# First batch in single query tiles, weight conversion spread from step 0, and the MLP's queue reordered, in a fused top-k attention and MLP kernel

## The chip, the cores and the metric

The kernel runs on one core of one Trainium2 chip. The metric is the device time of one execution in microseconds (us), and the time of the kernel before is the median of three runs. All steps and lines below name the kernel before, where nothing else is said.

## The reference, cut to what matters

```python
# q, k, v: (8 batches, 8 heads, 576 rows, 64)
scores = 0.125 * q @ k.T                      # 576 x 576 per head
kth = 32nd largest of each row
attn = softmax(where(scores >= kth, scores, -1e9))
x = (attn @ v), heads side by side            # (8, 576, 512)
xn = (x - mean) / sqrt(var + 1e-6) * g_ln     # over the 512
out = x + relu(xn @ w_ch1) @ w_ch2            # 512 -> 2048 -> 512
```

The weights arrive as 64-bit floats and are converted to 32 bits inside the kernel. All matrix products are in 32-bit floats; each appears in the trace as two matmul records and two weight loads.

## The kernel before, in words

The attention is cut into 160 **units**. A unit is one batch, one pair of heads and one tile of query rows. The 576 rows of a batch give four full tiles of 128 rows (numbers 0 to 3) and a last one of 64 (number J = 4, the "rest"). A full unit has two score tiles, one for each head; a rest unit packs both heads into one.

The units of one head pair and one set of query tiles form a **job**. The tiles of a job are one **group**: its product with the values (`values`, L487 and L494) is made at once, when the last unit is through. A batch has eight jobs: four head pairs for a first half of its tiles, then four for the second. Batch 0 has tiles 0, 1 and then 2, 3, J; the other batches have 0, 1, J and then 2, 3. So units 0 to 7 are full, and so on.

A loop runs over **steps** n. The instructions are written out by hand in that order, and each engine runs its own in that order (`manual_schedule`). In step n these run:

- TensorE (PE): scores of unit n+1 (L362), transposes of the weights of unit n-2 (L434, L463; L454, L455 for a rest), the values product of a group that ended with unit n-3, the transposes of its result (L526, `place`), and MLP work.
- VectorE (DVE): the 32 largest of unit n in four rounds of `select` (L379 max, L384 match-replace), the turning of heads (L321, `turn_heads`), the reciprocals of the softmax sums (L782).
- GpSimd (POOL): the mask of unit n-1 (L409, L412). While weights are converted, units are **shared** with ScalarE: then tile 0 of the unit gets its mask from two ScalarE activations (L399, L400) and one POOL operation (L407).
- ScalarE (ACT): copies of the scores from PSUM (L345), exponentials of unit n-2 (L419), copies and scalings.
- SyncE (SP): the DMA queue, in order.

**Weight conversion.** The weights are 32 pieces of 128x512: 16 of `w_ch1` (four column blocks `nb` with four pieces each) and then 16 of `w_ch2`. A piece goes through `fetch` (DMA), `split` (three ACT activations L168 to L172 and a POOL clamp L173), `shift` (DVE, L176) and `join` (two POOL operations, L182 and L183). When a column block is whole, `mean_of` (PE, L212) and `centre` (DVE, L223) fold the layer norm's mean and gain into it. `weights(n, phase)` is called at phases 0 to 3 of a step. Four pieces come ahead of the loop, then two with each step, and from step 10 one. `mean_of` is in phase 3, the end of a step, so it stands on PE ahead of the scores of the next step.

**The MLP.** Query tiles whose heads are all done make a **block** (mostly two tiles). `Block.items()` gives its work: `turn_x` (transposes of x, L576, copy L581), 64 `hidden` products (L589, as wide as the block) with an activation (L601) for each four, and 16 `project` products for each tile (L606, 512 wide). A block is handed over (`give`) four steps after its last unit. `give` first runs all that is left of the earlier blocks, then sets a plan: the block's cost is spread over the steps up to the next block. `fill()` has eight places in a step and puts as much of the list there as the plan allows.

Blocks are given at step 11, then 23, 35, 43, 55, 63, 75 and so on. The rests of two batches make a full tile of 128 rows; the rests of batches 0 to 3 make a block of two such tiles, given together with the block of step 75, and those of batches 4 to 7 one with the block of step 155. These two steps so hand over four tiles.

`NV` is the number of buffers of values (`v`, `ends`). `hpool` has 15 buffers of 128x512, for the conversion's temporaries and the activated hidden layer.

Of the kernel before, what the change touches and what calls it, by code (L numbers as in the profile page):

```python
# [20 lines left out]
J = 4  # L21
# [7 lines left out]
def kernel(  # L29
# [50 lines left out]

    NV = 3
    GQ = 2 * P + R
# [17 lines left out]
    xtpool = pool("xt", 1)  # L100
    hpool = pool("h", NF - 1)
    psps = pool("ps", 5, space=PSUM)
# [29 lines left out]
    class Piece:  # L132
# [26 lines left out]
        def split(self):  # L159
            def tmp(name, dt):  # L160
                return hpool.tile([P, DM], dt, tag="h", name=name)

            high = self.raw[:, :, 1].bitcast(FP32)
            self.size = tmp("size", U32)
            self.low = tmp("low", FP32)
            self.sign = tmp("sign", FP32)
            size_f = self.size[:].bitcast(FP32)
            nc.scalar.activation(size_f, high, AF.Abs)  # L168
            nc.scalar.activation(
                self.low[:], self.raw[:, :, 0], AF.Copy, bias=2.0, scale=2.0**-51  # L170
            )
            nc.scalar.activation(self.sign[:], high, AF.Sign)  # L172
            nc.gpsimd.tensor_scalar(size_f, size_f, HIGH_MAX, HIGH_MIN, ALU.min, ALU.max)  # L173
# [6 lines left out]
        def join(self):  # L180
            size = self.size[:]
            nc.gpsimd.tensor_tensor(size, size, self.low[:].bitcast(U32), ALU.add)  # L182
            nc.gpsimd.tensor_tensor(  # L183
                self.dst, size.bitcast(FP32), self.sign[:], ALU.mult
            )
            ready[self.i] = True

    ready = [False] * (2 * NF)
    centred = [False] * (DFF // DM)
    pieces = [Piece(i) for i in range(2 * NF)]  # L190
    gmat = [None]
    means = {}

    def load_gain():
        grow = const([NC, P], "grow")
        nc.scalar.dma_start(grow[:], g_ln.rearrange("(c p) -> c p", p=P))
        ps = turned()
# [22 lines left out]
    def centre(nb):  # L220
        for c in range(NC):
            w = w1[:, c, nb * DM : (nb + 1) * DM]
            nc.vector.scalar_tensor_tensor(  # L223
                out=w, in0=w, scalar=gcol[:, c : c + 1], in1=means[nb][:],
                op0=ALU.mult, op1=ALU.subtract,
            )
        centred[nb] = True

# [3 lines left out]
    for n in range(-1, 2 * NF):  # L232
        size = 4 if n < 0 else 2 if n < 10 else 1
        batches[n], queue = queue[:size], queue[size:]

    def weights(n, phase):

        now, before = batches.get(n, []), batches.get(n - 1, [])
        done = [x.i // NC for x in before if x.i < NF and x.c == NC - 1]
        if phase == 0:  # L240
            for x in batches.get(n + 1, []):
                x.fetch()
            for x in now[0::2]:
                x.split()
        elif phase == 1:
            for x in before:
                x.shift()
            for x in before[0::2]:
                x.join()
        elif phase == 2:  # L250
            for x in now[1::2]:
                x.split()
            for x in before[1::2]:
                x.join()
            for nb in means:
                if not centred[nb]:
                    centre(nb)
        elif phase == 3:
            for nb in done:
                mean_of(nb)  # L260

# [4 lines left out]
    owed = [0.0]  # L266

    def pop():
        cost, run, may = todo.pop(0)
        assert not may or may()  # L270
        owed[0] -= cost
        run()

    def fill():
        owed[0] = min(owed[0] + share[0], 6.0)
        while todo and owed[0] >= todo[0][0] / 2 and (not todo[0][2] or todo[0][2]()):
            pop()
# [9 lines left out]

    def load(job, other):

        job.ins = {}  # L290
        for name, src, queue in (("k", k, nc.sync), ("q", q, other)):
            t = ldpool.tile([P, S], FP32, tag=name + "in", name=name + "in")
# [46 lines left out]
    def scores(u):  # L339

        u.sc = scpool.tile([P, 2, S], FP32, tag="sc", name="sc")
        made = [score_half(u, s) for s in range(2)]
        for s, pss in enumerate(made):
            for t, ps in enumerate(pss):
                nc.scalar.copy(u.sc[:, t, s * HALF : (s + 1) * HALF], ps[:, 0:HALF])  # L345

# [191 lines left out]
    class Block:  # L538
# [25 lines left out]
        def items(self):  # L564
# [6 lines left out]
            def turn_x(i):  # L571
                if i == 0:
                    xT[0] = xtpool.tile([P, NC, 2 * P], FP32, tag="xT", name="xT")
                tp = turned()
# [28 lines left out]
            def project(i, f):  # L603
# [9 lines left out]
                if f == NF - 1:  # L613
# [5 lines left out]

            per_row = 1.75e-3  # L620
            out = [(0.66, lambda i=i: turn_x(i), None) for i in range(n)]
            out += [
                (
                    max(per_row * N, 0.31),
                    lambda f=f, c=c: hidden(f, c),
                    lambda f=f: centred[f * P // DM],
                )
                for f in range(NF)
                for c in range(NC)
            ]  # L630
            out += [
                (
                    per_row * DM,
                    lambda i=i, f=f: project(i, f),
                    lambda f=f: ready[NF + f] and (f < NF - 1 or self.ready),
                )
                for i in range(n)
                for f in range(NF)
            ]
            return out  # L640


# [5 lines left out]
    for b in range(B):  # L648
        lo, hi = list(range(J // 2)), list(range(J // 2, J))
        (lo if b else hi).append(J)  # L650
        for qts in (lo, hi):
            jobs += [Job(b, hp, [qts]) for hp in range(NHP)]
# [31 lines left out]
    for j in jobs:  # L684
        if j.hp == NHP - 1:
            b = j.b
            rest = J in j.groups[0].qts
            step = j.last + 4
            tiles = [(b, qt) for g in j.groups for qt in g.qts if qt < J]
            add_block(step, tiles, [[(out[b, t[1] * P : (t[1] + 1) * P, :], full)] for t in tiles])  # L690
            if b % 4 == 3 and rest:
                rests = [("r", b // 2 - 1), ("r", b // 2)]
                add_block(
                    step,
                    rests,
                    [
                        [
                            (out[2 * r, JP:S, :], slice(0, R)),
                            (out[2 * r + 1, JP:S, :], slice(R, P)),
                        ]  # L700
                        for _, r in rests
                    ],
                )

    SLOTS = 8
# [4 lines left out]
    turns = {}  # L710
    for j in fresh[1:]:
        before = jobs[jobs.index(j) - 1]
        turns[before.first] = j

# [20 lines left out]
    def give(n):  # L735
        while todo:
            pop()
        owed[0] = 0.0
        for blk in gives[n]:
            todo.extend(blk.items())  # L740
        after = [m for m in gives if m > n]
        steps = range(n, min(after) if after else END)
        need = sum(t[0] for t in todo)
        kappa = (need + sum(map(pe_cost, steps))) / sum(map(dve_cost, steps))
# [5 lines left out]

    load(fresh[0], nc.scalar)
    weights(-2, 0)
    turn_heads(fresh[0])
    load(fresh[1], nc.sync)
    scores(units[0])
    load_gain()
    load_values(jobs[0])
    weights(-1, 0)
    weights(-1, 2)
    recips = {}  # L760
    for n in range(END):
        if n in gives:
            give(n)
# [4 lines left out]
        late = late if late and late.rest and late.job.b % 2 else None  # L768
        if u and n == u.job.first and n > 0:
            load_values(u.job)  # L770
        parts = turn(ex) if ex else []
# [3 lines left out]
        if nxt:  # L775
            scores(nxt)
        if g:
            values(g)
        if u:
            select(u, 0)  # L780
        for den in recips.pop(n, []):
            nc.vector.reciprocal(den, den)  # L782
        if mk:
            prepare(mk)
            mask(mk, 0)
        weights(n, 0)
# [10 lines left out]
        if n in turns:  # L797
            turn_heads(turns[n])
            later = fresh.index(turns[n]) + 1
            if later < len(fresh):  # L800
                load(fresh[later], nc.sync)
        for blk in gives.get(n - 1, []):
            blk.std()
        if mk and len(mk.tiles) > 1:
            mask(mk, 1)
        weights(n, 1)
# [9 lines left out]
        if u:  # L816
            select(u, 2)
        for blk in gives.get(n - 1, []):
            blk.inverse()
        if ex and ex.group.last == n - 2:  # L820
            whole = [qt for qt in ex.group.qts if qt < J]
            den = ex.group.den[:, 2 * whole[0] : 2 * whole[-1] + 2]
            nc.gpsimd.tensor_scalar_add(den, den, DEN_EPS)
            recips.setdefault(n + 1, []).append(den)
        last_rest = at(n - 3)
# [7 lines left out]
        if parts:  # L833
            parts[-1]()
        fill()
        if u:
            select(u, 3)
# [5 lines left out]
        if late and late.job.hp == NHP - 1:  # L843
            r = late.job.b // 2
            blk, i = block_of["r", r]
            blk.stats(i, rs[r])
        weights(n, 3)
        fill()
# [33 lines left out]
```

## Time and profile before

| what | value |
|---|---|
| median of three runs | 1771.33 us (1771.23 to 1772.55) |
| profiled execution, device time | 1770.78 us |
| its span | 1768.3 us |
| PE busy | 1635.9 us (93%) |
| VectorE busy | 1521.8 us (86%) |
| GpSimd busy | 1208.3 us (68%) |
| ScalarE busy | 969.3 us (55%) |
| PE busy in the first 242 us | 145.9 us |
| VectorE's last unit ends | 1638.5 us |

The span is the profiler's, and 2.5 us of the execution lie around it. A matmul's end is modelled by the profiler, so that PE's work is best read from the starts of records in the timeline. Where a step begins on VectorE is read from the start of the first max over fresh scores of its unit. Where a block begins on PE is read from the first record of L576.

### The profile page before, as it was taken

What the parts mean: (1) busy time and instruction counts of PE and PEld (TensorE: products, weight loads), DVE (VectorE), ACT (ScalarE), POOL (GpSimd) and SP (SyncE); (2) the same over time, 40 slices, a digit from 0 to 9 for tenths busy, and PEclk for the clock granted to TensorE, in tenths of its full rate; (3) what the DMA queues carried; (4) which work ended last, traced back from release to release, by engine and by line L of the source; (5) the groups of instructions that cost most, each with busy time, mean ns of one, the idle gap of its engine ahead of it and who ended that gap; (6) DMA issues with size and microseconds to landing.
All of it is one profiled execution on the core that took longest, in us unless ns stands there. A gap on an engine that the chain in (4) does not pass through costs nothing.

```text
span 1768.3 us, 23805 instructions
## 1 busy us (share of the span) xinstructions
PE 1635.9 (93%) x7617; PEld 1034.6 (59%) x7617; DVE 1521.8 (86%) x3162; ACT 969.3 (55%) x2563; POOL 1208.3 (68%) x959
## 2 busy tenths in 40 slices
PE   3555999999999999999999999999999999999998
PEld 1223746657574757575756575647575756566765
DVE  7888999999999999996569999999999999996000
ACT  4658876556564646553356565656565646544411
POOL 4869787787777777873467877777778776883300
PEclk9677999999999999999999999999999999999999
DMA  7423112101210012001021012101120021000000
GB/s 173 103 69 97 54 31 51 28 26 28 46 28 20 24 37 54 20 14 38 15 39 28 26 28 53 21 20 27 34 53 21 20 40 34 14 26 14 6 13 12
DMA packets 244485, 65.53 MB, mean 37 GB/s; under 512 B 235653, under 2 KB 235657, under 8 KB 244361
## 3 DMA queue, kind: packets, MB, share of 16 engines
q1 hardware_dynamic: 241984, 63.73, 16.2%
q8 instruction: 60, 0.98, 0.2%
q10 hardware_dynamic: 2376, 0.30, 0.1%
q14 instruction: 65, 0.52, 0.1%
HBM read 54.53 MB, written 9.44 MB: 36 GB/s over the span
## 4 chain that ended last, share of the span: by engine, by line
DVE 41%; PE 35%; POOL 9%; issue 9%; ACT 5%; DMA 1%; POOLq 0%; SPq 0%; DVEq 0%; ACTq 0%
DVE m L379 21%; DVE wk L384 18%; PE hps L589 13%; PE ops L606 11%; PE scps L362 4%; PE av L487 3%; PE tp L434 3%; POOL e L409 2%; POOL w L183 2%; POOL size L182 2%; POOL e L412 2%; ACT sc L345 1%; POOL e L407 1%; PE av L494 1%; POOL size L173 1%
## 5 line engine op out<-in xcount | busy, mean ns | idle before, releaser
L409 POOL TENSOR_SCALAR e<-sc,m 128x576 f32<-128x576 f32 x270 | 598.2, 2215 | 239.4 <-DVE m L379 170.9
L379 DVE MAX8 m<-wk 128x8 f32<-128x576 f32 x864 | 612.6, 746 | 2.1
L589 PE MATMUL hps<-xT,w 128*128 128x256 f32 x2304 | 556.9, 385 | 27.5 <-ACT xT L581 27.5
L606 PE MATMUL ops<-w,h 128*128 128x512 f32 x1152 | 544.0, 596 | 0.0
L589 PEld LDWEIGHTS hps<-xT,w 128*128 128x128 f32 x2304 | 419.5, 192 | 93.8 <-ACT xT L581 31.8
L384 DVE MATCH_REPLACE8 wk<-m,wk 128x576 f32<-128x576 f32 x576 | 423.7, 742 | 0.0
L412 POOL TENSOR_TENSOR e<-e,sc 128x576 f32<-128x576 f32 x270 | 380.3, 1409 | 22.6
L606 PEld LDWEIGHTS ops<-w,h 128*128 128x128 f32 x1152 | 199.3, 191 | 162.5 <-issue 157.4
L419 ACT ACTIVATE e<-e,bias 128x576 f32<-128x576 f32 x288 | 225.3, 782 | 57.5 <-POOL e L412 55.4
L345 ACT COPY sc<-scps 128x288 f32<-128x288 f32 x576 | 191.8, 415 | 97.9 <-PE scps L362 94.7
L379 DVE MAX8 m<-sc 128x8 f32<-128x576 f32 x288 | 203.1, 742 | 40.1 <-ACT sc L345 40.0
L362 PE MATMUL scps<-kT,qT 64*128 64x288 f32 (+3 forms) x1344 | 223.1, 435 | 9.3 <-DVE qT L321 8.1
L446 ACT COPY pt<-tp 128x512 f32<-128x512 f32 x256 | 150.3, 588 | 138.3 <-PE tp L434 136.8
L434 PE MATMUL tp<-ident,e 128*128 128x128 f32 x1152 | 178.0, 278 | 49.8 <-ACT e L419 49.8
L434 PEld LDWEIGHTS tp<-ident,e 128*128 128x128 f32 x1152 | 143.7, 143 | 126.7 <-ACT e L419 62.4
L384 DVE MATCH_REPLACE8 wk<-m,sc 128x576 f32<-128x576 f32 x288 | 211.9, 742 | 0.0
L362 PEld LDWEIGHTS scps<-kT,qT 64*128 64x128 f32 (+1 forms) x1344 | 126.5, 182 | 131.0 <-issue 59.7
L601 ACT ACTIVATE h<-hps 128x256 f32<-128x256 f32 x288 | 110.4, 384 | 159.5 <-PE hps L589 158.6
L487 PE MATMUL av<-pt,vb 128*64 128x256 f32 (+1 forms) x1024 | 141.2, 419 | 0.3
L616 POOL TENSOR_TENSOR o<-o,x 128x512 f32<-128x512 f32 x32 | 40.7, 1273 | 126.0 <-ACT o L615 125.7
L487 PEld LDWEIGHTS av<-pt,vb 128*64 128x64 f32 x1024 | 69.2, 139 | 66.5 <-issue 19.7
L503 ACT ACTIVATE x<-xo,den 128x64 f32<-128x64 f32 x256 | 59.3, 316 | 72.4 <-DVE den L782 39.2
(71 smaller groups left out, 1020.9 us busy)
## 6 DMA issues: line engine op xcount, KB each, us to landing
raw<-in_moe_w_ch_dram SPq DMA_DIRECT2D x32, 512.0 KB, 3.9
vb<-in_v_dram SPq DMA_DIRECT2D x128, 128.0 KB, 2.4
kin<-in_k_dram SPq DMA_DIRECT2D x128, 72.0 KB, 2.4
qin<-in_q_dram SPq DMA_DIRECT2D x124, 72.0 KB, 2.4
out_dram<-o SPq DMA_DIRECT2D x32, 256.0 KB, 2.1
ends<-in_v_dram SPq DMA_DIRECT2D x128, 16.0 KB, 2.1
dr<-den SPq DMA_DIRECT2D x64, 0.2 KB, 1.8
out_dram<-o SPq DMA_DIRECT2D x8, 128.0 KB, 2.4
```

The lines of the kernel that those rows point to most:

```text
L345: nc.scalar.copy(u.sc[:, t, s * HALF : (s + 1) * HALF], ps[:, 0:HALF])
L362: nc.tensor.matmul(ps[i * R : i * R + ql, o : o + width], qT[r, q0 : q0 + ql], kT[r, k0 : k0 + width], start=True, stop=True,)
L379: nc.vector.max(m[:, t, :], u.cur[t])
L384: nc.vector.match_replace(u.wk[t][:], m[:, t, :], u.cur[t], LOWEST)
L409: nc.gpsimd.tensor_scalar(e, sc, u.thr[:, t, 7:8], MASKED, ALU.is_lt, ALU.mult)
L412: nc.gpsimd.tensor_tensor(e, e, sc, ALU.add)
L419: nc.scalar.activation(u.e[:, t], u.e[:, t], AF.Exp, bias=u.bias[:, t : t + 1], scale=scale, accum_out=g.den[:, col : col + 1],)
L434: nc.tensor.transpose(ps[:, c * P : (c + 1) * P], u.e[:, t, c * P + t * R : (c + 1) * P + t * R], ident[:],)
L446: nc.scalar.copy(g.pt[:, t * J : (t + 1) * J, q0 : q0 + P], ps[:].rearrange("p (c n) -> p c n", n=P),)
L487: nc.tensor.matmul(av[h * D : (h + 1) * D, 0 : g.nq], vb[:, h * J + c, :], g.pt[:, h * J + c, 0 : g.nq], start=(c == 0), stop=False,)
L589: nc.tensor.matmul(ps["h"][:, 0:N], w1[:, c, f * P : (f + 1) * P], xT[0][:, c, 0:N], start=(c == 0), stop=(c == NC - 1),)
L606: nc.tensor.matmul(ps["o"][:], hT[f][:, i * P : (i + 1) * P], w2[:, f, :], start=(f == 0), stop=(f == NF - 1),)
```

## The change

The diff does these things.

1. **Batch 0 in single tiles.** Its jobs are now tile 0, tile 1, tiles 2 and 3, and the rest alone, each for four head pairs. So it has 16 jobs, and its first two blocks have one tile, given at steps 7 and 11, and then one of two tiles at step 19. Batch 1 has tiles 0, 1 first and then 2, 3, J. From batch 2 on the halves are as before.
2. **Conversion.** No pieces ahead of the loop; two with each of steps 0 to 15. Clamps and shifts are moved (`shift` to phase 0, all `join`s to phase 1, ahead of the second `split`). `mean_of` moves from the end of step n to phase 1 of step n+1, `centre` follows it in phase 2. The sign tiles move to the pools `o` and `r`. Units 0 to 15 are shared, not 0 to 17. In a shared unit the mask of tile 1 is made ahead of that of tile 0.
3. **Start.** The heads of the second job are loaded through SP and ACT and turned ahead of the loop; the gain comes by SP, and its transposition is put into step 0 behind the scores. Later heads are turned up to two steps earlier. Values are loaded near the end of the step after a job's last unit, into two buffers instead of three.
4. **The MLP's queue.** At a new block only hidden products are run to the end; products of the earlier block stay in line, behind the new block's `turn_x`. While weights are still being converted, the hidden products of a new block go ahead of the earlier block's products, and every place gets 1.2 us.
5. **Rests.** The rests of two batches are the third tile of a block of the odd batch, given one step later: 3-tile blocks at steps 44, 76, 116 and 156.
6. A block's `inverse` is one step later; `hpool` has 16 buffers; the copies of scores go tile by tile.

```diff
-    NV = 3
+    NV = 2
...
-    hpool = pool("h", NF - 1)
+    hpool = pool("h", NF)
...
-            self.sign = tmp("sign", FP32)
+            pl, tag = ((opool, "o"), (rpool, "r"))[self.i % 2]
+            self.sign = pl.tile([P, DM], FP32, tag=tag, name="sign")
...
-        size = 4 if n < 0 else 2 if n < 10 else 1
+        size = 0 if n < 0 else 2
...
         if phase == 0:
             for x in batches.get(n + 1, []):
                 x.fetch()
+            for x in before:
+                x.shift()
             for x in now[0::2]:
                 x.split()
         elif phase == 1:
             for x in before:
-                x.shift()
-            for x in before[0::2]:
                 x.join()
-        elif phase == 2:
             for x in now[1::2]:
                 x.split()
-            for x in before[1::2]:
-                x.join()
+            for x in batches.get(n - 2, []):
+                if x.i < NF and x.c == NC - 1:
+                    mean_of(x.i // NC)
+        elif phase == 2:
             for nb in means:
-                if not centred[nb]:
+                if centred[nb] is None:
                     centre(nb)
-        elif phase == 3:
-            for nb in done:
-                mean_of(nb)
...
-        lo, hi = list(range(J // 2)), list(range(J // 2, J))
-        (lo if b else hi).append(J)
-        for qts in (lo, hi):
+        parts = [[0], [1], [2, 3], [J]]
+        if b:
+            parts = [[0, 1], [2, 3]]
+            parts[b < 2].append(J)
+        for qts in parts:
             jobs += [Job(b, hp, [qts]) for hp in range(NHP)]
...
-            if b % 4 == 3 and rest:
-                rests = [("r", b // 2 - 1), ("r", b // 2)]
+            if J in j.groups[0].qts and b % 2:
+                step += 1
+                tiles.append(("r", b // 2))
...
-    for j in fresh[1:]:
+    for j in fresh[2:]:
         before = jobs[jobs.index(j) - 1]
-        turns[before.first] = j
+        turns[min(before.first, j.first - 2)] = j
...
     def give(n):
-        while todo:
+        early = not all(map(done, ready))
+        while todo and not early and todo[0][0] != "project":
             pop()
         owed[0] = 0.0
         for blk in gives[n]:
-            todo.extend(blk.items())
+            rows, hidden, project = blk.items()
+            kept = [i for i in todo if i[0] != "project"]
+            last = [i for i in todo if i[0] == "project"]
+            if early:
+                todo[:] = kept + rows + hidden + last + project
+            else:
+                todo[:] = kept + rows + last + hidden + project
...
+        if early:
+            plan.update({m: 1.2 for m in steps})
+            return
...
-    load(fresh[1], nc.sync)
+    load(fresh[1], nc.sync, nc.scalar)
+    nc.sync.dma_start(grow[:], g_ln.rearrange("(c p) -> c p", p=P))
     scores(units[0])
-    load_gain()
-    load_values(jobs[0])
-    weights(-1, 0)
-    weights(-1, 2)
+    turn_heads(fresh[1])
+    load(fresh[2], nc.sync, nc.sync)
...
+            order = list(range(len(mk.tiles)))
+            if mk.shared:
+                order.reverse()
+            mask(mk, order[0])
...
-        for blk in gives.get(n - 1, []):
+        for blk in gives.get(n - 2, []):
             blk.inverse()
...
+        if mk and mk.job.last == n - 1:
+            load_values(mk.job)
...
-        weights(n, 3)
```

## The prediction

> **What bounds the kernel now.** I read the busy time by stretches first, because the page's mean of 93% for PE mixes stages. The columns are the stretch, its length, busy time (count) of PE, PE's weight loads, VectorE, ScalarE and GpSimd, then PE's granted clock, the DMA share and GB/s.
>
> ```profile
> 44.00:66.00 22.00, 8.45 (x16) 3.80 (x17) 21.50 (x41) 10.58 (x25) 20.50 (x16) 0.59 0.55 136
> 132.00:154.00 22.00, 11.84 (x56) 6.99 (x56) 16.62 (x33) 19.69 (x49) 20.80 (x18) 0.68 0.36 109
> 176.00:198.00 22.00, 20.70 (x105) 15.71 (x106) 20.42 (x44) 16.51 (x41) 16.68 (x14) 0.88 0.14 39
> ...
> 242.00:264.00 22.00, 22.00 (x99) 11.43 (x99) 21.83 (x47) 13.10 (x36) 17.75 (x15) 1.00 0.02 6
> ```
>
> Up to 176 us GpSimd sets the pace, and PE idles half the time. From 242 us on PE is nearly full. The same view, cut where blocks begin on PE:
>
> ```profile
> 575.20:662.20 87.00, 85.32 (x420) 55.42 (x419) 84.74 (x178) 49.49 (x130) 65.38 (x50) 1.00 0.15 31
> 662.20:762.90 100.70, 98.40 (x483) 61.61 (x481) 100.19 (x213) 59.87 (x168) 77.56 (x63) 1.00 0.16 33
> 762.90:907.20 144.30, 141.75 (x621) 92.85 (x620) 89.96 (x190) 58.84 (x154) 68.25 (x53) 1.00 0.11 22
> 907.20:1004.30 97.10, 95.51 (x481) 60.42 (x479) 96.58 (x202) 58.99 (x162) 76.90 (x60) 1.00 0.17 34
> ```
>
> Two tiles over 8 steps (first line) are PE's; two tiles over 12 steps (second) are VectorE's, busy 100.2 of 100.7; four tiles over 8 steps (third) leave VectorE idle for 54 us. Why the start is slow stands in the chain of waits (start, length, what):
>
> ```profile
> 63.74 1.34 POOL w L183
> 65.13 2.08 PE mean L212 x2
> 67.20 1.31 PE scps L362 x4
> 68.51 1.29 ACT sc L345 x4
> 69.99 0.72 ACT e L399
> 70.73 0.69 ACT e L400
> 71.50 1.41 POOL e L407
> ```
>
> GpSimd ends a join at 65.1 and idles until 71.5: the mean on PE waits for the join, the next scores stand behind the mean, ScalarE's mask activations behind those scores, and GpSimd needs them. It recurs every second step. Of the waits, three tell the same:
>
> ```profile
> ACT sc L345 <- PE scps L362: 94.7, 68, 12.8
> POOL e L407 <- ACT e L400: 43.0, 10, 6.8
> PE mean L212 <- POOL w L183: 29.4, 8, 9.7
> ```
>
> **Durations.** From starts in the timeline at full clock: 64 hidden products 256 wide 27.7 us (1707.9 to 1735.6), 32 output products 27.6; so a tile costs 27.65. Scores of a unit 1.17; its transposes 0.99; the values product of 256 columns 2.42, of 320 2.95; eight transposes of x 0.87. On VectorE a full unit is 9.64 (1010.41 to 1020.04), a rest 5.61 (949.33 to 954.94), a turned head pair 1.35 more. D(n) is the start of unit n on VectorE: D(2)=41.9, D(10)=162.1, D(19)=252.1, D(20)=257.7. So steps 2 to 9 take 15.0 each. P(n) is PE's start of a block given at step n: P(23)=282.7, P(43)=474.6.
>
> **Part 1, steps 0 to 18.** *Start.* The second head pair is turned ahead of the first max. Its load waits for the first turn (7.3), and the first load took 4.25 on the chain, so D(0) is some 13.5 instead of 10.9. The shifts of four early pieces leave step 0, so D(1) is 24.5 against 25.7.
>
> *The wait removed.* The mean now stands a step after its joins. GpSimd without the 6.4 us idle: a step with two pieces and a shared mask takes 11.7 to 11.9 (41.60 to 53.34, 144.37 to 156.23), with the sum of a group 12.3 (156.23 to 168.56). Single-tile groups have that sum in nearly every step; I take 12.2. VectorE needs 9.64, 0.75 for two shifts, and 2.7 for centring in four steps: 11.2 on average, so GpSimd is the bound. The reciprocal waits at 2.8 us into a step for a sum that ends GpSimd's step; as GpSimd is the bound, this sets its lag to 2.8 and costs nothing more. D(16)=24.5+15x12.2=207.5.
>
> *PE.* A single-tile hidden layer has 128 records of 128 columns. Eight transposes of that shape take 0.87, so 0.109 each is the low end (14 us); a weight load's own 0.190 the high end (24). They overlap, so I take 0.125: 16 us against 13.8. Small values products: 128 or 64 wide, between half of 2.42 and all of it, three more for each head pair against one of 320 less: 3 to 17 us in all. Steps 7 to 13 then hold 32 hidden, 7 means, 30 attention, 7 products: 76 us against 85 that GpSimd takes. Where PE was as full (176 to 198) it had a clock of 0.88, and 76 becomes 86. ScalarE has some 10.3 a step by its timeline (exponentials 1.7, copies 2.8, mask 1.9, splits 3.4, scalings 0.5) and 2 more in four of them. I add 4 us (ends 0, and 23 at a clock of 0.70, between the 0.59 and 0.77 of the stretches ahead of 176). D(16)=211.5.
>
> The Trainium skill, "TensorE: Matmul & The Clock Gate" (Part 1: The HAM clock gate), says that PE runs at half rate after an idle window of about 3.4 us, until it has been busy for one such window. The first ten hidden records at 177.3 took 0.43 each and later ones 0.22, which agrees. By the rule one gap in each of the seven steps would cost 1.7 us each, 12 us, and the sum below would be 8 us longer.
>
> *Other queues.* SP gets 32 more loads of values, and they wait for PE to free a buffer two jobs old; a load lands in 2.4 us and is issued more than one step (12 us) ahead of use. Weight fetches stand behind them, one step ahead too. If this cover failed, each of 15 steps would lose up to 2.4. The last three steps are rests: 16.8, a turn 1.35, a shift 0.75, and some 5 for a sum that GpSimd brings late. D(19)=236, 16 us earlier than before.
>
> **Part 2, steps 19 to 43.** VectorE: 19 full units (183.2), 6 rests (33.7), six turns (8.1), statistics and reciprocals (5): 231. PE's four tiles and attention come to 98 and 96 us in the two intervals, so VectorE bounds. D(44)=467. Where VectorE bounds, PE stands about 6 us ahead (1004.3 against D(95)=1010.4), so P(44)=461. Before, P(43)=474.6, and a step later makes it 485.
>
> **Part 3, from step 44.** Both kernels have 30 tiles left. The products "kept in line" change nothing here: the plan spends all of a block's cost by the next block, and in the changed program's order no product is left over at these. So each interval costs the larger of PE's and VectorE's work:
>
> - 44 to 55, three tiles: 83 + 1.3 + transposes 9.5 + scores 12.7 + values 11.8 + 1 = 119, with the wait for xT and 1.5% as in the lines above 122 (VectorE 95).
> - 76 to 83 and 116 to 123, three tiles, 7 steps: 107, so 110 each. 156 to 163: 100.5, so 103.
> - 63 to 76, 103 to 116, 143 to 156, two tiles, 13 steps: PE 100, VectorE 10x9.64+3x5.61+2x1.35+1=117. PE enters 1 us behind VectorE (1091.3 against D(103)=1090.0) and leaves 6 ahead, so 110 each. Ends: 106 (the largest swing seen is 11, between 907 and 1004) and 117 (none).
> - As before: 8 steps 87 (three times), 12 steps after a PE-bound stretch 97 (twice), the last block 62.
>
> The sum in order of time: 122+87+110+110+97+87+110+110+97+87+110+103+62=1292. Before: 1768.3-485=1283. So spreading the rests loses 9 us: three long intervals bound by VectorE cost what the two four-tile stretches gave.
>
> **Sum.** 461+1292=1753 of span, and 2.5 around it: 1756, against 1770.8 of the profiled execution, which stands 0.5 below the median of 1771.3.
>
> **The rivals.** *A: as above*, 1756; from D(19) of 228 to 244 and the long intervals' ends, 1740 to 1767.
>
> *B: the gain is kept in full.* GpSimd holds 11.8 (-6), no loss on PE (-4), long intervals 106 (-12): 1734. For it: 144 to 168 us, where GpSimd didn't stop. Against: PE is then nearly full with cold stretches.
>
> *C: no change.* The swing fails in two of three long intervals: +14, 1770. For it: 100.7 instead of 97 where a PE-bound stretch of 8 steps came before. Against: after 144 us of PE-bound work it was there in full.
>
> *D: slower.* The first sixteen steps become a lockstep of PE and ScalarE: each step has now a values product and its copy ahead of the mask's activations, and GpSimd waits for those at its 3.7th us. In the changed order ScalarE's next exponential stands some 10 to 14 us after the last, by transposes, scores and values at a cold clock of 0.6 to 0.7. It decides when the mean step from 1 to 16 passes 13.2; at 14.3 it costs 32 us: 1788. For it: the ScalarE row of 132 to 154 us, 19.7 of 22. Against: GpSimd has a lag of 2.8 and starts each step on the tile that needs no ScalarE.
>
> **How the numbers follow.** A 0.57, B 0.12, C 0.10, D 0.21. A measurement of this kernel tells 0.2% (3.5 us) from no change. A and B are faster: 0.69; C same: 0.10; D slower: 0.21. The likeliest case's own range is 1740 to 1767. With half of B's below 1732 and some of D's above 1786 left out, the range is 1732 to 1786.
>
> **What would show it.** Right: GpSimd's waits for ScalarE's mask (L400) fall from 43 us to under 15; D(10) is 134 to 142 and D(19) near 236; PE's first hidden record comes near 103 us; VectorE over 98% from step 19 to 44; blocks of three tiles take 110 to 122 with VectorE idle. Wrong: a step of over 13 us before 16 with ScalarE waiting for PE's values (D), long intervals of 115 or more (C), or a steady loss from 44 on, such as hidden products of three tiles slower than 0.65 us each pair of records.

## The result, and the profile after

The changed kernel takes 1791.71 us (median of 4 runs, 1791.03 to 1794.97) where the kernel before takes 1771.28 beside it: a ratio of 1.0117, 95% interval 1.0100 to 1.0135. It is 20 us slower. The forecast was 1756, 15 us faster. The profiled execution took 1791.03, its span 1789.2; the forecast's span was 461 + 1292 = 1753, so 36 us are to be found.

Line numbers of the changed kernel are some six higher: L595 is a hidden product, L612 an output product, L368 the scores, L582 the transposes of x, L170 to L175 the split of a piece, L184 and L185 its join, L561 the square root of a block's statistics, L178 the shift of a piece.

The stretches of the changed kernel that answer to those of before (stretch, length, busy time and count of PE, PE's weight loads, VectorE, ScalarE, GpSimd, then PE's clock, DMA share, GB/s):

```profile
44.00:66.00 22.00, 14.53 (x75) 9.09 (x73) 22.00 (x47) 16.10 (x41) 20.88 (x19) 0.78 0.41 127
66.00:88.00 22.00, 15.47 (x80) 9.31 (x80) 22.00 (x45) 16.47 (x45) 21.37 (x19) 0.81 0.43 123
88.00:110.00 22.00, 14.55 (x58) 10.28 (x59) 21.96 (x45) 16.35 (x37) 21.03 (x17) 0.56 0.37 99
110.00:132.00 22.00, 18.58 (x157) 15.54 (x156) 21.20 (x45) 17.84 (x47) 16.10 (x15) 1.00 0.29 86
132.00:154.00 22.00, 17.20 (x101) 11.00 (x99) 20.64 (x43) 19.71 (x53) 20.51 (x18) 1.00 0.34 105
...
176.00:198.00 22.00, 17.86 (x100) 13.41 (x101) 12.10 (x26) 18.27 (x46) 15.28 (x13) 0.92 0.21 61
198.00:220.00 22.00, 16.95 (x82) 9.26 (x81) 17.58 (x37) 18.91 (x47) 21.34 (x18) 0.84 0.36 99
220.00:242.00 22.00, 13.38 (x47) 6.12 (x44) 14.50 (x29) 9.13 (x25) 21.18 (x18) 0.84 0.00 1
242.00:264.00 22.00, 21.44 (x111) 11.98 (x109) 9.17 (x20) 9.06 (x26) 9.28 (x9) 1.00 0.16 42
```

From 44 to 110 us VectorE has no idle time, and GpSimd is busy for 20.9 us or more of each 22; up to 154 us VectorE stays at 20.6 or more, while GpSimd falls to 16.1 in one stretch. The forecast had GpSimd as the bound there. From 176 us on VectorE stands idle, for 10 of the 22 us to 198 and for 13 of those from 242 to 264. Before, it was busy 20.4 and 21.8 in these two. The same view, cut where blocks of two, two and three tiles begin on PE:

```profile
605.78:692.41 86.63, 85.34 (x420) 55.46 (x419) 75.84 (x159) 49.56 (x130) 63.25 (x47) 1.00 0.16 31
692.41:806.35 113.94, 109.04 (x519) 67.22 (x518) 113.39 (x242) 66.61 (x186) 88.89 (x73) 0.97 0.14 29
806.35:916.11 109.76, 108.23 (x421) 58.99 (x419) 75.31 (x158) 46.75 (x115) 55.84 (x42) 1.00 0.12 27
```

The 13 steps of the second line are VectorE's (113.4 of 113.9) and leave PE 5 us idle; the first and third are PE's.

In the table D(n) is the start of unit n on VectorE and P(44) PE's start of the block given at step 44. The forecast's D(13) is worked out by its terms, 24.5 + 12 x 12.2 + 4.

| | D(1) | D(10) | D(13) | D(16) | D(19) | D(44) | P(44) | span from P(44) |
|---|---|---|---|---|---|---|---|---|
| before | 25.7 | 162.1 | 193.4 | - | 252.1 | 484.3 | - | - |
| forecast | 24.5 | 134 to 142 | 174.9 | 211.5 | 236 | 467 | 461 | 1292 |
| changed | 25.6 | 140.1 | 174.5 | 221.4 | 261.5 | 490.7 | 483.55 | 1305.7 |

At unit 13 the kernel is on the forecast, 19 us ahead of before (where one of the first 13 units is a rest; here none is). At unit 19 it is 9 us behind before. The error of 36 is 22.5 at P(44) and 13.7 behind it. The first part arises in steps 13 to 18: 10.3 in steps 13 to 15 and 15.6 in steps 16 to 18; some 3 of this come back up to P(44). Two places stand out.

**Steps 13 and 14** take 35.0 us together. The chain of waits of the changed kernel there (start, length, what):

```profile
174.96 0.55 ACT size L170
175.51 0.56 ACT low L171
176.06 0.56 ACT sign L174
176.63 0.17 ACT h L607
176.84 0.49 PE hps L595 x2
...
178.40 1.28 ACT L561
...
186.09 1.80 PE hps L595 x16
187.92 0.28 ACT h L607
188.21 1.28 ACT L425
...
192.78 0.31 issue
193.09 0.68 ACT size L170
193.85 0.61 POOL size L175
```

PE's hidden products of the second one-tile block wait for the activation L607, which stands on ScalarE behind the splits of a piece; ScalarE then waits for PE's products, and does two table loads between. GpSimd's clamp L175 waits 6.31 us for a split, up to 193.85. VectorE loses the time by way of GpSimd: a shift waits for a clamp in step 13, and the reciprocal waits for a sum in step 14 (from three timelines, VectorE's, GpSimd's and VectorE's again):

```profile
183.54 0.43 DVE L178 TENSOR_SCALAR size<-size 128x512 uint32<-128x512 uint32 x1 [5.67 <-POOL size L175]
...
193.85 0.61 POOL L175 TENSOR_SCALAR size<-size 128x512 f32<-128x512 f32 x1 [6.31 <-ACT size L170]
...
201.91 0.18 DVE L801 RECIPROCAL den<-den 128x4 f32<-128x4 f32 x1 [8.05 <-POOL den L847]
```

From 193.85 to 237.03 us the chain is GpSimd's work alone, so its lost time here stands ahead of the join that PE waits for in step 18.

**Step 18** takes 25.0 us, though its unit is a rest. PE's timeline in the changed kernel (start, length, engine, line, operation, count, and in brackets the idle time before it and what ended it):

```profile
227.61 1.19 PE L368 MATMUL scps<-kT,qT 64*64 64x288 f32 x10
234.50 2.08 PE L612 MATMUL ops<-w,h 128*128 128x512 f32 x2 [5.70 <-POOL w L185]
237.07 7.94 PE L612 MATMUL ops<-w,h 128*128 128x512 f32 x14 [0.49 <-POOL w L185]
...
245.29 3.60 PE L612 MATMUL ops<-w,h 128*128 128x512 f32 x8
...
250.13 2.74 PE L612 MATMUL ops<-w,h 128*128 128x512 f32 x6
252.80 1.20 PE L368 MATMUL scps<-kT,qT 64*64 64x288 f32 x10
...
258.49 0.38 PE L532 MATMUL xo<-ident,oT 128*128 128x128 f32 x2
```

An output product waits for GpSimd's join of its piece of `w_ch2`. Then 16 products (32 records) run ahead of the scores of unit 19 (L368, the second time), and two more ahead of the transposes of a result (L532), which ScalarE scales (L509) and VectorE takes the statistics of (L557). On VectorE those stand ahead of unit 19's first max. VectorE's timeline in the changed kernel:

```profile
259.88 0.69 DVE L557 BATCH_NORM_STATS2 st<-x 128x6 f32<-128x512 f32 x1 [11.82 <-ACT x L509]
```

### The profile page after: what moved, and what is told of

It is laid out like the page before. It is cut to its first block, busy times and chain, and to the rows that moved or that the text cites. A ratio compares the mean times of both kernels' runs of the same rounds, so it can differ in the third digit from the quotient of the medians.

```text
span 1789.2 us, 23917 instructions
## 1 busy us (share of the span) xinstructions
PE 1652.8 (92%) x7633; PEld 1011.9 (57%) x7633; DVE 1515.6 (85%) x3165; ACT 972.3 (54%) x2548; POOL 1218.5 (68%) x966
## 4 chain that ended last, share of the span: by engine, by line
PE 43%; DVE 41%; issue 7%; ACT 5%; POOL 3%; DMA 1%; ACTq 0%; DVEq 0%; POOLq 0%
DVE m L385 21%; DVE wk L390 17%; PE hps L595 16%; PE ops L612 14%; PE scps L368 4%; PE av L493 3%; PE tp L440 3%; PE av L500 1%; POOL e L415 1%; ACT e L425 1%; ACT sc L349 1%; ACT xT L587 1%; DVE qT L325 1%; DVE kT L325 1%; POOL w L185 1%
## 5 line engine op out<-in xcount | busy, mean ns | idle before, releaser
L415 POOL TENSOR_SCALAR e<-sc,m 128x576 f32<-128x576 f32 x272 | 606.6, 2230 | 236.9 <-DVE m L385 180.5
L385 DVE MAX8 m<-wk 128x8 f32<-128x576 f32 x864 | 620.4, 764 | 2.0
L595 PE MATMUL hps<-xT,w 128*128 128x256 f32 (+2 forms) x2176 | 563.0, 401 | 37.0 <-ACT xT L587 29.0
L612 PE MATMUL ops<-w,h 128*128 128x512 f32 x1152 | 553.7, 606 | 11.0 <-POOL w L185 11.0
L595 PEld LDWEIGHTS hps<-xT,w 128*128 128x128 f32 x2176 | 381.7, 194 | 137.2 <-ACT xT L587 33.2
L390 DVE MATCH_REPLACE8 wk<-m,wk 128x576 f32<-128x576 f32 x576 | 428.8, 761 | 0.0
L612 PEld LDWEIGHTS ops<-w,h 128*128 128x128 f32 x1152 | 201.9, 193 | 182.4 <-issue 162.6
L368 PE MATMUL scps<-kT,qT 64*128 64x288 f32 (+3 forms) x1344 | 231.9, 435 | 52.8 <-DVE qT L325 31.8
L368 PEld LDWEIGHTS scps<-kT,qT 64*128 64x128 f32 (+1 forms) x1344 | 127.7, 180 | 177.6 <-issue 74.4
L607 ACT ACTIVATE h<-hps 128x256 f32<-128x256 f32 (+2 forms) x272 | 107.7, 398 | 157.0 <-PE hps L595 155.4
L493 PE MATMUL av<-pt,vb 128*64 128x256 f32 (+3 forms) x1152 | 146.3, 394 | 3.3 <-DMA vb<-in_v_dram 2.9
L493 PEld LDWEIGHTS av<-pt,vb 128*64 128x64 f32 x1152 | 76.7, 141 | 68.7 <-issue 25.1
L509 ACT ACTIVATE x<-xo,den 128x64 f32<-128x64 f32 x256 | 59.8, 317 | 70.7 <-DVE den L801 43.1
```

The costliest lines, as they stand in the source:

```text
L368: nc.tensor.matmul(ps[i * R : i * R + ql, o : o + width], qT[r, q0 : q0 + ql], kT[r, k0 : k0 + width], start=True, stop=True,)
L385: nc.vector.max(m[:, t, :], u.cur[t])
L390: nc.vector.match_replace(u.wk[t][:], m[:, t, :], u.cur[t], LOWEST)
L415: nc.gpsimd.tensor_scalar(e, sc, u.thr[:, t, 7:8], MASKED, ALU.is_lt, ALU.mult)
L493: nc.tensor.matmul(av[h * D : (h + 1) * D, 0 : g.nq], vb[:, h * J + c, :], g.pt[:, h * J + c, 0 : g.nq], start=(c == 0), stop=False,)
L595: nc.tensor.matmul(ps["h"][:, 0:N], w1[:, c, f * P : (f + 1) * P], xT[0][:, c, 0:N], start=(c == 0), stop=(c == NC - 1),)
```

## The experiments

The theories have numbers. For steps 13 to 18: **T1**, the pace is the cause, since 1.2 us in every place puts too much MLP work ahead of the scores; **T2**, it is not. For the time from step 44 on: **T3**, PE and VectorE bound it in turn since the last rows are third tiles given a step later; **T4**, that is not the cause. For the removed wait, taken alone: **T5**, it is worth what the sum says; **T6**, it is hidden. For single tiles: **T7**, they matter little; **T8**, they carry much of the gain. T9 to T11 came up on the way. All ratios are to the kernel before, run on the same chip, with 95% intervals.

### Half the pace

```diff
-            plan.update({m: 1.2 for m in steps})
+            plan.update({m: 0.6 for m in steps})
```

> The changed kernel with one number changed: while weights are converted, each place gets 0.6 us of MLP work instead of 1.2. Theory T1 (the loss before step 19 comes from too much MLP work put into steps 11 to 18: hidden products in lockstep with ScalarE in steps 13 and 14, 17 us, and products that wait for joins and then run ahead of the scores in step 18, 25 us): VectorE starts unit 19 near 240 us instead of 261.5, some 13 products go to the steps from 19 on where PE has room, and the time falls to 1767 to 1775. Rival T2 (single-tile groups, with a values product and a sum in each step, are what slows the steps): unit 19 still starts after 255 us and the time stays at 1785 to 1792.

Measured: 1771.00 us, 1.0000 (0.9991 to 1.0009). T1 holds: 20.7 us come back. Two stretches of this run:

```profile
176.00:198.00 22.00, 16.97 (x114) 13.72 (x115) 19.52 (x45) 21.02 (x56) 19.59 (x17) 0.92 0.20 63
...
220.00:242.00 22.00, 19.22 (x108) 10.89 (x108) 18.02 (x36) 11.67 (x32) 20.30 (x19) 1.00 0.27 54
```

GpSimd is busy 19.6 of 22 us in the first where it was 15.3, and PE 19.2 in the second where it was 13.4: less work in each place gives more work done. Steps 13 and 14 take 23.4, step 18 11.8. D(19) is 238.4 and P(44) 460.4, where the forecast had 236 and 461. So P(44) comes 23.1 us sooner than in the changed kernel; the span is 19.9 shorter, and 3.2 are lost again behind step 44.

### Output products only from step 19 on

```diff
-                        lambda f=f: done(ready[NF + f]) and ...
+                        lambda f=f: now[0] >= 19 and ...
```

> The changed kernel with the output products of the two single-tile blocks held back until step 19. Hidden products stay where they are. T1: the 17 us of steps 13 and 14 stay, the 25 us of step 18 fall to under 10, and 32 products (27.5 us) move to steps 19 to 30, where PE has some 19 us of room and so pays 8: time 1775 to 1782. T2: no gain, 1788 to 1800.

Measured: 1783.43, 1.0068 (1.0051 to 1.0085), 1.4 us over T1's range. Step 18 falls to 11.8 (under 10 was expected), and D(19) to 244.4. But the interval from the block of step 19 to that of step 31 grows from 109.7 to 123.3: the postponed products fill PE there, which is busy 123.3 of 123.3 us. Steps 13 and 14 still take 30.0.

### Half the pace from step 15 on only

```diff
-            plan.update({m: 1.2 for m in steps})
+            plan.update({m: 1.2 if m < 15 else 0.6 for m in steps})
```

> The changed kernel with 1.2 us a place up to step 14 and 0.6 us from step 15 on, so that steps 7 to 14 stay as they are and only the rush of products in steps 15 to 18 is slowed. T1 says that there are two losses, one in steps 13 and 14 and one in step 18, and that they add up: D(15) stays at 208 to 211 us, step 18 falls from 25.0 to 12 to 15 us, D(19) is 247 to 252, the block of step 44 begins on PE at 469 to 475, and the time is 1777 to 1784 us. T9, that the first loss is not one of its own, as GpSimd's work of steps 15 to 18 would end no earlier without it: D(19) is 238 to 243 and the time 1768 to 1774, as with 0.6 us throughout. T2, that the pace is not the cause: 1788 to 1795.

Measured: 1792.32, 1.0115 (1.0098 to 1.0132): as the changed kernel. My theory fell, for step 18 takes 21.0 still, and the 2.9 us that P(44) gains are lost again behind it. The pace of steps 15 to 18 is not the main cause. I read it so: the products come right behind their joins because the hidden products have been used up early. These end and output products follow at 190.0 us in the changed kernel, and at 203.0, two steps later, with half the pace throughout. From then on each place takes the piece that was joined a step before in the program, and GpSimd, busy 21.2 of 22, ends that join late. And a place that finds its product not yet allowed keeps its share: `fill` saves up to 6.0 us, which are spent in one go in step 18. This gave two more runs, for the **wait** and for the **savings**.

### The same, and nothing saved up

```diff
-        owed[0] = min(owed[0] + share[0], 6.0)
+        owed[0] = min(owed[0] + share[0], 0.6 if 15 <= now[0] < 19 else 6.0)
```

> As the run with 1.2 us a place up to step 14 and 0.6 us from step 15, and in steps 15 to 18 the places save nothing up while the next output product has to wait (a place's 0.6 us is lost instead of being kept up to 6.0 us). So step 18 has 7 output products fewer ahead of the scores of unit 19. T10 says that step 18 loses by both: the wait of the products for GpSimd's joins, which stays, and the saved-up products behind it, some 6 x 0.94 us, which go: the step takes 14 to 16.5 us instead of 21, D(19) is 252 to 255, and as those products come in steps 19 to 30, where VectorE bounds, the time is 1784 to 1790 us. T11, that the wait alone makes the loss: the step stays at 19 to 22 us and the time at 1790 to 1795.

Measured: 1784.27, 1.0075 (1.0058 to 1.0092). Step 18 takes 13.7 us (T10: 14 to 16.5), D(19) is 250.0 (T10: 252 to 255), so T10's order of size holds and T11 falls. The savings cost 7.3 us of that step. PE's timeline in this run:

```profile
227.61 1.19 PE L368 MATMUL scps<-kT,qT 64*64 64x288 f32 x10
234.31 2.07 PE L612 MATMUL ops<-w,h 128*128 128x512 f32 x2 [5.50 <-POOL w L185]
...
237.02 3.43 PE L612 MATMUL ops<-w,h 128*128 128x512 f32 x4
...
240.84 1.02 PE L612 MATMUL ops<-w,h 128*128 128x512 f32 x2
241.79 1.20 PE L368 MATMUL scps<-kT,qT 64*64 64x288 f32 x10
...
247.49 0.38 PE L532 MATMUL xo<-ident,oT 128*128 128x128 f32 x2
```

The wait is there still, 5.50 us, but 8 records stand ahead of the scores, in place of 22 in the run before and 32 in the changed kernel, and L532 comes 11.0 us sooner than in the latter.

### A product only two steps after its join

```diff
-                        lambda f=f: done(ready[NF + f]) and ...
+                        lambda f=f: done(ready[NF + f]) and ready[NF + f] < now[0] - 1 and ...
```

> The changed kernel with an output product allowed only when its piece of w_ch2 was joined two steps before, not one. T10 says that PE then meets joins that are long done: its waits for L185 (11.0 us, of these 5.7 in step 18) go, step 18 falls from 25.0 to 12 to 15 us and D(19) is 247 to 252; the postponed products come as a rush from step 19 on, as in the run with products from step 19 on, so that steps 19 to 30 take 110 to 120 us, and the time is 1777 to 1787. T11, that a step's delay of the waiting changes nothing, as GpSimd's joins are late anyway: D(19) over 256 and 1788 to 1795.

Measured: 1780.11, 1.0055 (1.0040 to 1.0070). PE's matmuls no longer wait for L185 (11.0 us in the changed kernel), D(19) is 247.0 and steps 13 and 14 take 29.4, 5.6 less. Step 18 takes 16.3, a little over the 12 to 15 expected: the savings are now spent behind the scores of unit 19, but 22 records (234.6 to 244.5) are still ahead of L532, and VectorE's statistics wait 4.33 us for it by way of L509. So wait and savings each have a part, and half of the loss of steps 13 and 14 goes with the postponed products too.

### The rests as before

```diff
-            if J in j.groups[0].qts and b % 2:
-                step += 1
-                tiles.append(("r", b // 2))
...
+            if b % 4 == 3 and J in j.groups[0].qts:
+                rests = [("r", b // 2 - 1), ("r", b // 2)]
+                add_block(step, rests, ...)
```

> The changed kernel with the rests as in the kernel before: two-tile blocks of rests given with the blocks of steps 75 and 155, no third tile and no step added. Theory T3 (three-tile blocks alternate with 13-step intervals that VectorE bounds at 114 to 115.5, and these cost 14 us more from step 44 on than the kernel before): time 1774 to 1779. Rival T4 (PE's total alone decides, the place of the rests is worth nothing): 1789 to 1793.

Measured: 1774.21, 1.0014 (1.0005 to 1.0023). T3 holds: 17.5 us come back, all but 1 of them behind step 44, for D(44) is 489.7 against 490.7. Two stretches of this run, cut at the blocks of steps 63, 75 and 83:

```profile
669.16:769.82 100.66, 98.37 (x483) 61.68 (x481) 100.18 (x213) 60.34 (x168) 77.62 (x63) 1.00 0.16 33
769.82:912.88 143.06, 141.38 (x620) 93.06 (x619) 89.69 (x190) 59.24 (x154) 68.20 (x53) 1.00 0.11 23
```

They sum to 243.7 for 20 steps and six tiles. The changed kernel takes 223.7 for the same steps (692 to 916) and five tiles; with a sixth at 27.65 it would be 251.4, so the arrangement of before is 7.7 us the cheaper in this stretch.

### The kernel before, with the mean a phase later

In the kernel before, only `mean_of` is moved, from the end of the step with its joins to phase 1 of the next step. All lines from there on stand one lower.

```diff
+            for x in batches.get(n - 2, []):
+                if x.i < NF and x.c == NC - 1:
+                    mean_of(x.i // NC)
...
-        elif phase == 3:
-            for nb in done:
-                mean_of(nb)
```

> The kernel before with one edit: the product for the mean is put a step later, into phase 1, so that it no longer stands ahead of the scores while it waits for a join. Theory T5 (that wait costs 6.4 us in every second step): unit 10 starts at 138 to 145 us instead of 162.1 on VectorE, unit 20 near 238 instead of 257.7, and the time falls by 10 to 20 to 1751 to 1761. Rival T6 (GpSimd and PE take the gain back before step 23): 1768 to 1772.

Measured: 1748.86, 0.9873 (0.9859 to 0.9888), 2 us better than T5's range: 22.5 us from one line's place. Of the waits of this run (us in total, times, longest):

```profile
POOL e L406 <- ACT e L399: 21.5, 8, 5.1
...
PE mean L212 <- POOL w L183: 9.5, 5, 3.7
```

GpSimd waited 43.0 and the mean 29.4 before. D(10) is 142.7 in place of 162.1.

### Both repairs together, and without single tiles

The first is half the pace and the rests as before in one kernel; the second is the same with batch 0 in pairs.

> Both repairs in one kernel: 0.6 us a place while weights are converted, and the rests in pairs. If the two losses are independent they add: 20.7 and 17.5 us off 1791.7, so 1751 to 1757. If they share a cause (PE's total), only one of the two shows: 1768 to 1774.

Measured: 1749.99, 0.9885 (0.9871 to 0.9900). The gains of 20.7 and 17.5 would give 1753.5, so they add up (with 3.5 over), and two separate causes are shown.

```diff
-        parts = [[0], [1], [2, 3], [J]]
+        parts = [[0, 1], [2, 3], [J]]
```

> The kernel with both repairs, but batch 0 in tiles 0, 1 and 2, 3 and the rest, so no single-tile groups and blocks. Theory T7 (what is won at the start is the wait removed, and single tiles give nothing): within 5 us of the kernel with both repairs. Rival T8 (single tiles bring PE work forward that would be missed): 8 us or more slower than it.

Measured: 1753.79, 0.9904 (0.9888 to 0.9921). With the two repairs, single tiles are worth 3.8 us. The kernel before with the one moved line (1748.86) is as fast as the whole change with both repairs: up to here, the rest of the change has brought nothing over that line.

### Hidden work carried over a block

The queue that keeps products "in line" at a new block does something only if the plan leaves some over. Here the plan of an 8-step block runs two steps past its end (one, in the second kernel). The first is made on half the pace, the second on both repairs.

```diff
-        steps = range(n, min(after) if after else END)
+        end = min(after) if after else END
+        steps = range(n, end + 2 if end - n == 8 else end)
```

> The changed kernel with 0.6 us a place, rests as third tiles, and one edit: the plan of a block with eight steps to the next is spread over ten, so that 15 products (13 us) stay in line and run in the 13-step interval behind, where PE has room. T3 (the long intervals are VectorE's, with PE idle): the three 8-step intervals fall from 87 to 76 to 80, the long ones stay at 114 to 117, and the time falls from 1771.0 by 18 to 27 to 1744 to 1753. T4 (PE's total decides): 1769 to 1773.

Measured: 1751.77, 0.9891 (0.9876 to 0.9906), 19.2 us under half the pace alone. Its stretches from the block of step 55 to those of steps 63 and 76:

```profile
581.31:657.50 76.19, 74.15 (x390) 50.93 (x388) 75.71 (x159) 48.49 (x131) 63.33 (x48) 0.98 0.17 32
657.50:771.97 114.47, 114.42 (x550) 69.58 (x549) 113.48 (x242) 67.55 (x185) 88.88 (x72) 1.00 0.15 31
```

The 8 steps fall from 86.6 to 76.2 and are VectorE's now; the products go into the 13 steps, where PE had been idle for 6.5 us with half the pace and is full now (114.42 of 114.47). The other two pairs miss T3's ranges: their 8 steps take 81.0, and their 13 steps 118.4.

> Both repairs, and the plan of an eight-step interval spread over nine, so that 8 products (7 us) run in the 12-step interval behind. T3: 8-step intervals fall from 87 to 80 to 82, 12-step ones rise by at most 3, and the time is 6 to 16 us under the kernel with both repairs. T4: no change against it.

Measured: 1736.45, 0.9804 (0.9789 to 0.9819), 13.5 us under both repairs. The 8-step intervals of two tiles fall to between 80.5 and 82.4, and the 12-step ones behind them rise by 1.6 to 4.6, where at most 3 was expected; the first of four tiles falls from 143.1 to 129.0, and the 12 steps behind it rise by 12.0. It is the best version: 34 us faster than the kernel before and 55 than the changed one.

## Why the prediction was wrong

**Right: the wait removed.** GpSimd's wait for the mask activation (43 us) is gone from the changed kernel's waits, and so is PE's mean's; D(10) and D(13) are where the sum had them. Moved alone, the mean is worth 22.5 us. That the two starts fit is in part luck. The sum has GpSimd as the bound at 12.2 a step and VectorE at 11.2. The steps from 2 to 9 took 12.7, and VectorE is the engine without idle time from 44 to 110 us: its shifts took 0.80 us each in place of 0.75 for two, and all four centrings, 2.7 each, fall into these eight steps, where the sum spread them over fifteen. The 4 us added for PE made up for most of it.

**Failed: Part 1, "*PE.* ... I add 4 us (ends 0, and 23 ...)".** This sum took PE's and GpSimd's work for steps 7 to 13 and ended there; for these steps it fits (174.5 against 174.9). Steps 13 to 15 got GpSimd's 12.2 each, and "the last three steps are rests: 16.8 ...". The hidden products of both one-tile blocks are in it (32 us), but as busy time that fits beside GpSimd's, with nothing for their order behind ScalarE's splits; and nothing is charged for the output products that follow in steps 14 to 18, when a place's 1.2 us has used up the hidden ones. What the runs put there: 11.6 us in steps 13 and 14 (35.0 against 23.4 with half the pace) and 13.2 in step 18 (25.0 against 11.8). A busy time that fits in the stretch says nothing of the order in it: products of a piece just joined make PE wait for GpSimd's newest result, and the next scores wait behind them. That is the wait the change had removed from the mean, and it came back at another line. What is late next was asked of the reciprocal and the loads, not of `project`.

**Rival D had the sign, and part of the mechanism.** PE and ScalarE do go in lockstep, but in two steps, not sixteen. The mean step from 1 to 16 is 13.05 us, (221.4 - 25.6) / 15, short of the 13.2 from which D was to decide. Its price of 32 us in the first sixteen steps was not paid there: the loss against the forecast's D(16) is 9.9. That its 1788 lies near the 1791.7 measured is luck: most of the loss came in step 18 and behind step 44.

**Failed: Part 3, "PE enters 1 us behind VectorE ... and leaves 6 ahead, so 110 each".** The mechanism, VectorE as the bound of 13 steps, is right, the size is not: 113.9, 115.5 and 113.9, in sum 13.4 over, and all but 0.3 of the 13.7. By the starts, VectorE's 13 steps are 118.6 (D(63) = 691.1 to D(76) = 809.7) for the 117 of the sum. PE enters 1.3 us behind VectorE, as forecast (P(63) = 692.4), but leaves 3.4 ahead (P(76) = 806.35) and in the second such interval 1.8, not 6. So the swing is 3.0 to 4.7 us, not 7. Rival C named this ("the swing fails in two of three long intervals"); it half failed in all three. That "spreading the rests loses 9 us" became 17.5, by the run with the rests as before.

**Right: Part 2 and the rest of Part 3.** From unit 19 to 44 VectorE is busy 228.0 of 229.2 us, for 231 in the sum (whose terms add up to 230). In Part 3, 122.2, 86.6, 109.8, 97.9, 87.0, 109.8, 97.9, 87.0, 101.7 and 62.3 were measured for 122, 87, 110, 97, 87, 110, 97, 87, 103 and 62. "The products kept in line change nothing here" holds, and the run with carried products shows what it left: with another plan they are worth 13.5 to 19 us.

**Clock and table loads.** From PE's timeline in the changed kernel:

```profile
158.34 2.93 PE L595 MATMUL hps<-xT,w 128*128 128x128 f32 x12 [4.55 <-ACT xT L587]
...
185.93 1.95 PE L595 MATMUL hps<-xT,w 128*128 128x128 f32 x16
```

The first 12 one-tile records after PE's wait of 4.55 us took 0.244 each, the 16 at 185.9 took 0.122, near the 0.125 of the sum. So half the pace after an idle stretch is seen, as the rule that the prediction cites has it; its 8 us more would have been too little and at the wrong steps. ScalarE's change of tables is seen on the chain at 178.40 and 188.21, 1.28 us each. The Trainium skill, "ScalarE: Activation LUTs" (What ACT_TABLE_LOAD costs), says that a switch takes about 2.66 us, of which 1.38 are a drain. Here the copy ahead of it ends at 178.40, the load starts there, and the next activation starts at 179.69: no drain, and half the price.

**Open.** How the 11.6 us of steps 13 and 14 divide between ScalarE's order (splits and table loads ahead of L607), PE's clock (0.84 to 0.92 there) and the products that wait was not separated; the two runs with postponed products gave 5.0 and 5.6 of it. Nor is it shown why the time behind P(44) differs, from 1305.7 to 1310.6 us, among runs that are the same from there on: by this, a gain ahead of step 44 didn't arrive whole.

## What to carry to other kernels

When a wait is taken off an engine's queue, look for the next instruction there that needs the newest result of the engine that is the bound, and put a step's distance between them; here one move of a line was worth 22.5 us, and a step's distance at another line, where the same pattern had come up, 11.6. Work that fills gaps should be rationed to what its sources can supply: here a filler that went too fast used up its reserve, then ran in lockstep with its source, and shares saved up in that time came as a burst ahead of the critical work. Where two engines are the bound in turn, let work run over from one stretch into the next; that was worth 19.2 and 13.5 us in the two kernels where it was tried.

## What the runs showed of the hardware

A switch of ScalarE's tables cost 1.28 us with no drain seen, as told above. PE's granted clock was 0.56 in the changed kernel's stretch of 88 to 110 us, with PE busy 14.55 of 22, and 1.00 at 18.58 of 22 in the next; as VectorE was busy 21.96 of 22 in the first, nothing shows that the low clock cost anything there.
